# W_in in runs of 256 columns, and x of blocks 1 and 2 in another DMA ring

## The chip, the cores and the metric

The kernel runs on one core of one Trainium2 chip. The metric is device time in microseconds of one execution, the median over several. A core has five engines that run their own instruction streams and meet only through semaphores: TensorE (PE; its weight loads are listed as PEld), VectorE (DVE), ScalarE (ACT), GpSimd (POOL) and SyncE (SP). DMA transfers are issued from an engine's stream. Those that GpSimd issues go through a ring whose descriptors software writes (queue q0 in the profile, "software_dynamic"); those of SyncE and ScalarE go through two rings of the hardware (q1 and q10). All are carried out by the same sixteen DMA engines of the core, and each of the sixteen adds one to the transfer's semaphore when its share has landed. So a wait for 16 is a wait for one whole transfer.

## The reference

A short causal convolution along the sequence with softmaxed taps (8 heads of 24 channels, 7 taps), then a feed-forward layer with the exact GELU:

```python
def _attn_ref(x, weight):                 # x (8, 4096, 192), weight (8, 7)
    w = softmax(weight, axis=-1)
    x_pad = zeros(6 rows) + x             # along the sequence, per batch
    out[b, s, h, g] = sum_k w[h, k] * x_pad[b, s + k, h, g]

def _moe_ref(x, w_in, w_out):             # x (32768, 192), w_in (192, 2048), w_out (2048, 192)
    h = x @ w_in
    g = 0.5 * h * (1.0 + erf(h / sqrt(2)))
    return g @ w_out
```

Here the reference is written shorter than it stands; inputs and output are float32.

## The kernel before

**Tiling.** The 32768 tokens are cut into two halves of 16384, and the two are worked on side by side: half 0 lives in partitions 0 to 63, half 1 in partitions 64 to 127. The 192 channels are three groups (`NP`) of 64. A block is a run of tokens in both halves: blocks 0 to 5 have 256 tokens of each half, the others 512 (`WS`). The 2048 hidden columns are 16 chunks of 128; a chunk pair covers 256 columns, one chunk the even ones and one the odd.

**Stages of a block.** Its x is loaded (`load`, four transfers, by half and by half of the channels) into one of three `xin` buffers. VectorE turns it so that channels lie on partitions (`trans`, line 504). For blocks 0 and 1 the convolution is made on TensorE (`pconv`, line 686) from a bf16 copy (`cast`, by ScalarE for block 0, by GpSimd for block 1) with diagonal weights `dg`; `conv_out` takes it out of PSUM. From block 2 on VectorE makes it, in seven taps with two operations each (lines 525 and 532), the last of which write `xc`. Then `mm1` (line 741) multiplies with W_in into PSUM, ScalarE makes the GELU into `gT` (line 654), and `mm2` (line 772, or `mm2_t`, line 802, for blocks 6 and up) multiplies with W_out. In TensorE's stream the mm2 of the block before stands between the mm1 groups ("units") of a block; a block of 256 tokens has 8 units of two chunks each.

**W_in.** A matmul of a half reads its weights from the same partitions as its tokens, so both halves of the partitions need all of W_in (bf16, converted by the transfer). To read it from memory once, each half is given one part, and VectorE copies it to the other half (`dup`). The parts come in two stages. Before, half 0 owns columns 0 to 1023 and half 1 columns 1024 to 2047; stage 0 is the first 512 columns of each, stage 1 the rest, in runs of 512 columns (2 KB in memory). Half 1 keeps its columns rotated by 1024 (`wcols`). `CH` gives the order in which each half takes the chunks: units 0 and 1 of block 0 need only the half's own stage 0, units 2 and 3 the other half's copied stage 0, units 4 and 5 the stage 1 of half 0 and its copy, units 6 and 7 the stage 1 of half 1 and its copy. The waits for `S_WIN` and `S_DUPE` in `mm1` say this. W_out comes in four parts (`S_WOUT`), each with four chunks. With this `CH` the first sixteen steps of mm2 of block 0 have to be taken in the order `UO`, so that each four of them need one part of W_out.

**Order of the transfers before.** GpSimd's stream: two W_in transfers of stage 0; two of block 1's x (semaphore `S_XP[0]`); wait for the taps (`S_PRO` 9) and the larger part of the diagonal weights (line 397); the other two of block 1's x; two W_in transfers of stage 1; four of W_out; then halo and casts of block 1; four of block 2's x (`S_XP[1]`); halo of the later blocks. SyncE's stream: the taps' weights, half of block 0's x (ScalarE issues the other half); a wait until all of block 2's x has landed (`S_XP[1]`, 64); block 3's x; then, block by block, later x and stores.

**Order of VectorE before.** After the taps: transposes of block 0, its share of `conv_out`, both copies of stage 0 (`dup(0)`), transposes of block 1, both copies of stage 1 (`dup(1)`), `conv_out` of block 1, transposes of block 2, and so on. TensorE does the convolution of block 1 behind the mm1 of units 3 to 6 of block 0:

```python
behind = {(0, 3): p01[:6], (0, 4): p01[6:12], (0, 5): p01[12:] + p2[:6], (0, 6): p2[6:]}
```

Of the kernel before, what the change touches and what calls it, by code (L numbers as in the profile page):

```python
# [11 lines left out]
def bass_lightweight_conv__then__act_gelu_exact_kernel(  # L12
# [9 lines left out]
    D2, F = moe_w_in.shape  # L22
# [60 lines left out]

    CH = [[(8 * hf * (i < 8) + 8 * (i // 4 % 2) + 4 * (i // 8) + i % 4) % NF for i in range(NF)] for hf in range(2)]
    assert all(WS[n] == TB for n in range(M0, NB)) and NG[NB - 1] == 4 and SL0[NB] % 2 == 0

    OUTS = []
# [18 lines left out]
    with es:  # L108
# [24 lines left out]
        S_WIN = [sem("S_WIN%d" % i) for i in range(3)]  # L133
        S_WOUT = [sem("S_WOUT%d" % i) for i in range(4)]
        S_XIN = [sem("S_XIN%d" % i) for i in range(NX)]
        S_XP = [sem("S_XP%d" % i) for i in range(2)]
        S_OUT = [sem("S_OUT%d" % i) for i in range(2)]
        S_MSET = sem("S_MSET")
        S_WNM = sem("S_WNM")
# [69 lines left out]
                e.wait_ge(S_PCE, len(PV) + (1, 3, 6)[p])  # L209

        NCV = 2 * KS
        FH = F // 2
        FP = [0, FH // 2, FH]

        UO = [0, 1, 4, 5, 2, 3, 6, 7]
        UO += [u + 8 for u in UO]

        def cast(e, n, p):
            e.wait_ge(S_TR, NP * n + p + 1)
# [14 lines left out]
            return sum(NCV - 2 * (m in K0) for m in range(n + 1) if m not in PC)  # L234


        def wcols(hf, f):

            return f if hf == 0 else (f + FH) % F

        def xin_at(n):

            return 64 * (n // NX + (n % NX == 0))

        def banks(m, g):

# [122 lines left out]

        @block.gpsimd  # L370
        def _(g):
            def win_in(c0, c1, sm):
                for hf in range(2):
                    g.dma_start(  # L374
                        ap(win, 64 * hf * NP * F + c0, [[NP * F, 64], [F, NP], [1, c1 - c0]]),
                        ap(wint, hf * FH + c0, [[NP * F, 64], [F, NP], [1, c1 - c0]]),
                    ).then_inc(sm[hf], 16)

            g.wait_ge(S_MSET, 1)
            for hf in range(2):  # L380
                m = idb[64 * hf : 64 * hf + 64, :]
                g.affine_select(  # L382
                    out=m,
                    in_=m,
                    compare_op=ALU.is_equal,
                    fill=0.0,
                    base=0,
                    pattern=[[-1, 64]],
                    channel_multiplier=1,
                ).then_inc(S_IDN)  # L390
            g.wait_ge(S_IDN, 2)
            g.memset(wnm[:, :], 0.0).then_inc(S_WNM)  # L392
            g.memset(ap(xTb[0], HF, [[NP * XB, 128], [XB, NP], [1, HB]]), 0.0).then_inc(S_HALO)  # L393
            win_in(FP[0], FP[1], [S_WIN[0]] * 2)
            load(g, 1, (0, 2), S_XP[0])
            g.wait_ge(S_PRO, 9)
            g.tensor_tensor(
                ap(dg, 3 * 64, [[KS * 64, 128], [64, KS - 3], [1, 64]]),
                ap(idb, 0, [[64, 128], [0, KS - 3], [1, 64]]),
                ap(wcol, 3, [[32, 128], [1, KS - 3], [0, 64]]),  # L400
                ALU.mult,
            ).then_inc(S_DG)
            load(g, 1, (1, 3), S_XP[0])
            win_in(FP[1], FP[2], S_WIN[1:])
            for k in range(4):
                g.dma_start(
                    ap(wout, 2 * k * C, [[NF * C, 128], [8 * C, 2], [1, 2 * C]]),
                    ap(woutt, 256 * k * C, [[2 * C, 128], [1024 * C, 2], [1, 2 * C]]),
                ).then_inc(S_WOUT[k], 16)

            def halo(n):

                t, tw = (xTb[PC[n]], XB) if n in PC else (xT[n % 2], XW)
                dst = ap(t, HF, [[NP * tw, 128], [tw, NP], [1, HB]])
                if n >= 4:
                    g.wait_ge(S_CV, cvd(n - 2))
                if OFF[n] % SEQ == 0:
                    g.memset(dst, 0.0).then_inc(S_HALO)
                    return
                g.wait_ge(S_TR, trd(n - 1))  # L420
                src = ap(
                    xT[(n - 1) % 2], HF + WS[n - 1], [[NP * XW, 128], [XW, NP], [1, HB]]
                )
                g.tensor_copy(dst, src).then_inc(S_HALO)  # L424

            halo(1)
            for p in range(NP):
                cast(g, 1, p)
            load(g, 2, sm=S_XP[1])
            halo(2)  # L430
            for n in range(3, NB):
                halo(n)

        @block.vector
        def _(v):
# [22 lines left out]
                    ap(wnt, 4 * (q % 2), [[32, 32], [1, 4], [0, 8]]),  # L458
                ).then_inc(S_PRO)

            def dup(s):

                if s == 0:
                    v.wait_ge(S_WIN[0], 32)
                for hf in range(2):
                    if s == 1:
                        v.wait_ge(S_WIN[1 + hf], 16)
                    v.tensor_copy(
                        ap(
                            win,  # L470
                            64 * (1 - hf) * NP * F + FH + FP[s],
                            [[NP * F, 64], [F, NP], [1, FP[s + 1] - FP[s]]],
                        ),
                        ap(
                            win,
                            64 * hf * NP * F + FP[s],
                            [[NP * F, 64], [F, NP], [1, FP[s + 1] - FP[s]]],
                        ),
                    ).then_inc(S_DUPE)

            def trans(n, p):

                w = WS[n]
                if p == 0:
                    v.wait_ge(S_XP[n - 1] if n in (1, 2) else S_XIN[n % NX], 64 if n in (1, 2) else xin_at(n))
                    if n >= 2 and n - 2 in PC:
                        wait_pc(v, n - 2, NP - 1)
                    elif n >= 2:
                        v.wait_ge(S_CV, cvd(n - 2))
                    if n >= 2:  # L490
                        v.wait_ge(S_HALO, n)
                if n in PC:
                    out = ap(xT[n], p * XW + HX, [[NP * XW, 128], [1, w]])
                    src = ap(
                        xin[n % NX], p, [[TB // 32 * DQ, 128], [DQ, w // 32], [NP, 32]]
                    )
                else:
                    out = ap(xT[n % 2], HX, [[NP * XW, 128], [XW, NP], [1, w]])
                    src = ap(
                        xin[n % NX],  # L500
                        0,
                        [[TB // 32 * DQ, 128], [1, NP], [DQ, w // 32], [NP, 32]],
                    )
                v.transpose(out, src).then_inc(S_TR)  # L504
# [50 lines left out]
                trans(0, p)  # L555
            for j in PV:
                conv_out(v, 0, j)
            dup(0)
            for p in range(NP):
                trans(1, p)  # L560
            dup(1)
            for j in range(len(pieces(1))):
                conv_out(v, 1, j)

# [100 lines left out]
        def _(t):  # L665
# [41 lines left out]
            def mm1(n, i):  # L707
# [19 lines left out]
                for cc, p in todo:  # L727
                    if i == 0 and cc == 0 and p == NP - 1:
                        if n in PC:
                            wait_pc(t, n, p)  # L730
                        else:
                            t.wait_ge(S_CV, cvd(n))
                    for hf in range(2):
                        r = slice(64 * hf, 64 * hf + 64)
                        ch = CH[hf][i * c + cc]
                        f0 = 256 * (ch // 2) + ch % 2
                        fw = 64 if (n == 0 and 4 <= i <= 6) or M0 < n <= M1 else 128
                        for fo in range(0, 128, fw):
                            f1 = 64 * hf * NP * F + p * F + wcols(hf, f0) + 2 * fo
                            o = hf * TB + cc * w  # L740
                            ins = t.matmul(  # L741
                                hp[u % 2][fo : fo + fw, o : o + w],
                                ap(win, f1, [[NP * F, 64], [2, fw]]),
                                xc[n % 2][r, p * TB : p * TB + w],
                                start=(p == 0 and (cc == 0 or not head)),
                                stop=(p == NP - 1 and (cc == c - 1 or not head)),
                                tile_position=(64 * hf, fo),
                            )
                ins.then_inc(S_MM1)

            def mm2(m, g, ph, k):

                i = UO[k] if m == 0 else k
                w = WS[m]
                bb = banks(m, g)
                if k == 0:
# [4 lines left out]
                if g == 0 and ph == 0:  # L761

                    c = NCH[m]
                    if k % 4 == 0:
                        us = range(k, k + 4) if m else UO[k : k + 4]
                        t.wait_ge(S_GELU, SL0[m] + max(us) // c + 1)
                for hf in range(2):
                    sub = ph ^ hf
                    s = 2 * g + sub
# [57 lines left out]
            for n in range(NB):  # L827
                todo = units(n - 1) if n >= 1 else []
                for i in range(NSL[n]):
# [5 lines left out]
                    a0 = len(todo) * sum(ws[:i]) // sum(ws)  # L835
                    a1 = len(todo) * sum(ws[: i + 1]) // sum(ws)
                    for un in todo[a0:a1]:
                        if n == 1 and un[:2] == (0, 0) and un[2] % 4 == 0:
                            t.wait_ge(S_WOUT[un[2] // 4], 16)
                        (mm2_t if new else mm2)(n - 1, *un)  # L840
            m = NB - 1
            for g2 in range(0, NG[m], 2):
# [6 lines left out]
        def _(sp):  # L849
            sp.dma_start(wsb[:, :], ap(wt, 0, [[KS, H], [1, KS]])).then_inc(S_WSB, 16)  # L850
            load(sp, 0, (0, 1))

            sp.wait_ge(S_XP[1], 64)
            load(sp, 3)
            for n in range(1, NB):
                if n + 3 < NB:
# [34 lines left out]
```

## Time and profile before

| what | value |
|---|---|
| median of 4 runs | 681.05 us (680.62 to 682.66) |
| profiled execution, its own time | 680.56 us |
| its span | 678.8 us |
| GELU (line 654) | 512 of 1023 ns on average |
| W_in transfers | 4 of 192 KB (written), median 5.1 us from issue to landing |
| W_out transfers | 4 of 192 KB (written), median 6.9 us |
| x by GpSimd's ring | 8 of 96 KB, median 4.5 us |
| x by SyncE's ring, blocks of 256 tokens | 14 of 96 KB, median 2.4 us |
| granted TensorE clock | 1.00 in each of the first stretches of 8 us |

The span runs from the first to the last instruction that the profiler saw; the 1.76 us by which the execution's own time is longer lie around it. A line of a group names line, engine, operation, what is written from what is read, shapes, and the number of instructions. In the timeline, the first number is the start and the second the length in microseconds, and brackets hold the idle time of the engine before it, with what ended it. An engine name with a small q is the engine's sequencer, which issues transfers. Matmul ends are modelled, so neighbouring lines of TensorE overlap a little.

### The profile page before, as it was taken

To read this page: it belongs to the slowest core of one execution; us is meant where nothing else is said; L and a number is where in the kernel's file an instruction comes from. 1 tells how busy PE (TensorE), PEld (TensorE's weight loads), DVE (VectorE), ACT (ScalarE), POOL (GpSimd) and SP (SyncE) were. 2 spreads that over 40 slices of the span, in tenths; PEclk is the share of its full clock that TensorE was granted. 3 is DMA by queue.
4 is the path that set the end of the run, shared out by engine and by line. 5 is a ranking of instruction groups with operands and counts; after the bars stand their busy time and mean duration, and the time that the engine had idled before them with its cause. 6 is when DMAs were issued, how large, how long until landed. Compare 5 with 4: busy or idle time off the path is not lost.

```text
span 678.8 us, 27140 instructions
## 1 busy us (share of the span) xinstructions
PE 673.7 (99%) x12644; PEld 413.8 (61%) x12644; DVE 527.4 (78%) x607; ACT 536.5 (79%) x550; POOL 35.7 (5%) x62
## 2 busy tenths in 40 slices
PE   8999999999999999999999999999999999999998
PEld 7999655555555555555555555555555555555557
DVE  6989977977779877779777788777797777887511
ACT  8899978787777787787877777877877777778772
POOL 7010000000000000000000000000000000000000
DMA  9335324224443234442234431244422344410123
GB/s 162 98 96 131 71 60 96 53 50 90 95 96 75 52 66 96 95 96 55 51 87 96 95 86 41 65 96 95 96 59 50 84 96 95 92 44 11 48 50 95
DMA packets 131585, 53.66 MB, mean 79 GB/s; under 512 B 125328, under 2 KB 131344, under 8 KB 131472
## 3 DMA queue, kind: packets, MB, share of 16 engines
q1 hardware_dynamic: 128048, 48.97, 31.9%
q0 software_dynamic: 2304, 2.36, 2.1%
q8 instruction: 99, 1.62, 1.0%
q10 hardware_dynamic: 1120, 0.59, 0.3%
q14 instruction: 14, 0.11, 0.1%
HBM read 28.31 MB, written 25.17 MB: 79 GB/s over the span
## 4 chain that ended last, share of the span: by engine, by line
PE 98%; DMA 1%; ACT 1%; POOL 0%; issue 0%; DVE 0%
PE hp L741 49%; PE ob L802 43%; PE ob L772 5%; DMA win<-in_moe_w_in_dram 1%; PE hp L772 1%; ACT gT L654 1%; POOL win L374 0%; POOL idb L382 0%; PE ob L686 0%; DVE osb L293 0%; DVE idb L436 0%; POOL wnm L392 0%; POOL xTb L393 0%
## 5 line engine op out<-in xcount | busy, mean ns | idle before, releaser
L654 ACT ACTIVATE gT<-hp 128x1024 bf16<-128x1024 f32 x512 | 522.7, 1023 | 129.0 <-PE hp L741 125.7
L741 PE MATMUL hp<-xc,win 64*64 64x512 bf16 (+3 forms) x6084 | 419.1, 366 | 1.5 <-DMA win<-in_moe_w_in_dram 0.7
L802 PE MATMUL ob<-gT,wout 64*64 64x512 bf16 x5376 | 366.6, 377 | 0.0
L532 DVE SCALAR_TENSOR_TENSOR acc<-xT,wcol,acc 128x1024 f32<-128x1024 f32 (+1 forms) x330 | 295.6, 947 | 2.9 <-ACT acc L627 2.9
L741 PEld LDWEIGHTS hp<-xc,win 64*64 64x64 bf16 (+1 forms) x6084 | 188.8, 106 | 134.4 <-ACT gT L654 2.0
L802 PEld LDWEIGHTS ob<-gT,wout 64*64 64x64 bf16 x5376 | 173.9, 119 | 121.4
L324 DVE STREAM_TRANSPOSE osb<-ob 128x512 f32<-128x512 f32 x84 | 74.0, 884 | 129.4 <-PE ob L802 129.4
L504 DVE STREAM_TRANSPOSE xT<-xin 128x1536 f32<-128x1536 f32 (+2 forms) x39 | 74.7, 1923 | 1.7 <-DMA xin<-in_x_dram 1.6
L532 DVE SCALAR_TENSOR_TENSOR xc<-xT,wcol,acc 128x1024 bf16<-128x1024 f32 (+1 forms) x66 | 60.4, 954 | 0.0
L424 POOL COPY xT<-xT 128x18 f32<-128x18 f32 x30 | 22.6, 754 | 512.2 <-DVE xT L504 489.6
L772 PE MATMUL ob<-wout,gT 64*128 64x192 bf16 x896 | 46.8, 243 | 0.0
L772 PEld LDWEIGHTS ob<-wout,gT 64*128 64x128 bf16 x896 | 38.7, 94 | 5.1 <-issue 0.4
L525 DVE TENSOR_SCALAR acc<-xT,wcol 128x512 f32<-128x512 f32 (+2 forms) x60 | 33.7, 604 | 1.1
L295 ACT ACTIVATE osb<-ob 128x192 f32<-128x192 f32 x2 | 0.7, 330 | 7.1 <-PE ob L772 7.1
L772 PE MATMUL hp<-wout,gT 64*128 64x192 bf16 x128 | 5.9, 243 | 0.0
L668 PE MATMUL hp<-const-bfloat16-1.0 128*128 128x128 bf16 x48 | 5.0, 301 | 0.8 <-PEq L876 0.8
L293 DVE COPY osb<-ob 128x192 f32<-128x192 f32 x2 | 0.7, 358 | 6.1 <-PE ob L772 6.1
L668 PEld LDWEIGHTS hp<-const-bfloat16-1.0 128*128 128x128 bf16 x48 | 4.9, 142 | 0.8 <-issue 0.8
L772 PEld LDWEIGHTS hp<-wout,gT 64*128 64x128 bf16 x128 | 5.3, 94 | 0.0
L627 ACT ACTIVATE acc<-xT,wcol 128x256 f32<-128x256 f32 (+1 forms) x9 | 5.2, 579 | 0.0
L280 ACT ACTIVATE osb<-ob 128x384 f32<-128x384 f32 x10 | 4.9, 486 | 0.0
L337 POOL DMA_DIRECT2D xin<-in_x_dram x8 | 4.8, 629 | 0.0
(36 smaller groups left out, 32.6 us busy)
## 6 DMA issues: line engine op xcount, KB each, us to landing
out_dram<-osb SPq DMA_DIRECT2D x124, 192.0 KB, 3.1
xin<-in_x_dram SPq DMA_DIRECT2D x116, 192.0 KB, 4.0
xin<-in_x_dram SPq DMA_DIRECT2D x14, 96.0 KB, 2.4
win<-in_moe_w_in_dram POOLq DMA_DIRECT2D x4, 192.0 KB, 5.1
xin<-in_x_dram POOLq DMA_DIRECT2D x8, 96.0 KB, 4.5
wout<-in_moe_w_out_dram POOLq DMA_DIRECT2D x4, 192.0 KB, 6.9
out_dram<-osb ACTq DMA_DIRECT2D x4, 96.0 KB, 2.2
out_dram<-osb SPq DMA_DIRECT2D x4, 96.0 KB, 2.6
```

Source lines behind the costliest of these rows:

```text
L280: e.activation(out=dst, in_=src, func=AF.Copy).then_inc(S_EVA)
L324: v.transpose(ap(osb[m % 2], j, [[8 * C, 128], [C // 2, TB // 32], [NP, 32]]), bank(ring(m, j)),).then_inc(S_EV)
L424: g.tensor_copy(dst, src).then_inc(S_HALO)
L504: v.transpose(out, src).then_inc(S_TR)
L525: ins = v.tensor_scalar(a, src, wk, None, ALU.mult)
L532: ins = v.scalar_tensor_tensor(dst, src, wk, a, op0=ALU.mult, op1=ALU.add)
L627: a.activation(out=acc[n % 2][:, p * TB : p * TB + w], in_=ap(xT[n % 2], p * XW + HX, [[NP * XW, 128], [1, w]]), func=AF.Copy, scale=wcol[ ...
L654: a.activation(out=ap(gT[n % 2], i * c * 2 * w, dst), in_=ap(hp[u % 2], 0, src), func=AF.Gelu,).then_inc(S_GELU)
L668: t.matmul(hp[1][:, 0:128], one, one)
L741: ins = t.matmul(hp[u % 2][fo : fo + fw, o : o + w], ap(win, f1, [[NP * F, 64], [2, fw]]), xc[n % 2][r, p * TB : p * TB + w], start=(p == ...
L772: ins = t.matmul(bb[sub], gT[m % 2][r, c0 : c0 + 128], wout[r, CH[sub][i] * C : (CH[sub][i] + 1) * C], start=(ph == 0 and k == 0), stop=(p ...
L802: ins = t.matmul(bank(ring(m, j), slice(64 * h, 64 * h + 64), w), ap(wout, 64 * hf * NF * C + CH[h][i] * C + j, [[NF * C, 64], [NP, 64]],) ...
```

## The change

Half `hf` now owns, in stage `s`, columns 256 * (2s + hf) to 256 * (2s + hf) + 255 and the same 1024 further on, for each of the three channel groups: six runs of 256 columns (1 KB in memory, 512 B as bf16) per partition, where there were three of 512. The columns lie at the same place in both halves, so `wcols` goes. `CH` is made to fit, and with it mm2 of block 0 takes the chunks in their own order (`UO` goes); its first eight steps need the first two parts of W_out, which are waited for together.

GpSimd's ring carries only weights: two of stage 0, the first of stage 1, (the diagonal weights), the second of stage 1, four of W_out. Block 1's x is issued by SyncE after `S_PRO` 9, and block 2's after the third part of W_out has landed; block 3's follows without a wait of its own on a landing. `S_XP` goes. On VectorE the copies are single steps, and the first of stage 1 stands ahead of the transposes of block 1.

```diff
-    CH = [[(8 * hf * (i < 8) + 8 * (i // 4 % 2) + 4 * (i // 8) + i % 4) % NF for i in range(NF)] for hf in range(2)]
+    CH = [
+        [4 * (i // 8) + 2 * ((i // 4 + hf * (i < 8)) % 2) + 8 * (i // 2 % 2) + i % 2 for i in range(NF)]
+        for hf in range(2)
+    ]
...
+        FQ = F // 8
+        def part(s, hf):
+            return FQ * (2 * s + hf), [[NP * F, 64], [4 * FQ, 2 * NP], [1, FQ]]
...
-            def win_in(c0, c1, sm):
-                for hf in range(2):
+            def win_in(s, sm, hfs):
+                for hf in hfs:
+                    c0, pat = part(s, hf)
                     g.dma_start(
-                        ap(win, 64 * hf * NP * F + c0, [[NP * F, 64], [F, NP], [1, c1 - c0]]),
-                        ap(wint, hf * FH + c0, [[NP * F, 64], [F, NP], [1, c1 - c0]]),
+                        ap(win, 64 * hf * NP * F + c0, pat), ap(wint, c0, pat)
                     ).then_inc(sm[hf], 16)
...
-            win_in(FP[0], FP[1], [S_WIN[0]] * 2)
-            load(g, 1, (0, 2), S_XP[0])
+            win_in(0, [S_WIN[0]] * 2, (0, 1))
+            win_in(1, S_WIN[1:], (0,))
             g.wait_ge(S_PRO, 9)
...
-            load(g, 1, (1, 3), S_XP[0])
-            win_in(FP[1], FP[2], S_WIN[1:])
+            win_in(1, S_WIN[1:], (1,))
...
-            load(g, 2, sm=S_XP[1])
             halo(2)
...
-            dup(0)
+            dup(0, 0)
+            dup(0, 1)
+            dup(1, 0)
             for p in range(NP):
                 trans(1, p)
-            dup(1)
+            dup(1, 1)
...
-                            f1 = 64 * hf * NP * F + p * F + wcols(hf, f0) + 2 * fo
+                            f1 = 64 * hf * NP * F + p * F + f0 + 2 * fo
...
-                i = UO[k] if m == 0 else k
+                i = k
...
-                        us = range(k, k + 4) if m else UO[k : k + 4]
-                        t.wait_ge(S_GELU, SL0[m] + max(us) // c + 1)
+                        t.wait_ge(S_GELU, SL0[m] + (k + 4) // c)
...
-                        if n == 1 and un[:2] == (0, 0) and un[2] % 4 == 0:
-                            t.wait_ge(S_WOUT[un[2] // 4], 16)
+                        if n == 1 and un[:2] == (0, 0) and un[2] in (0, 8, 12):
+                            for q in {0: (0, 1), 8: (2,), 12: (3,)}[un[2]]:
+                                t.wait_ge(S_WOUT[q], 16)
...
-            sp.wait_ge(S_XP[1], 64)
+            sp.wait_ge(S_PRO, 9)
+            load(sp, 1)
+            sp.wait_ge(S_WOUT[2], 16)
+            load(sp, 2)
             load(sp, 3)
```

## The prediction

> **What bounds the kernel now.** I read the page first (busy shares, the forty slices, the chain that ended last), then the chain in order of time over the first 20 us, then the timeline of each engine there, then single DMAs from issue to landing.
>
> ```profile
> span 678.8 us, 27140 instructions
> PE 673.7 (99%) x12644; PEld 413.8 (61%) x12644; DVE 527.4 (78%) x607; ACT 536.5 (79%) x550; POOL 35.7 (5%) x62
> PE   8999999999999999999999999999999999999998
> ```
>
> TensorE is at 99%, and only its first slice (17 us) is less than full. The whole run's list of TensorE's waits holds 1.2 us on data (0.7 on W_in, 0.5 on the GELU), all before 17 us. The change leaves every matmul in number and shape, so the time can move only by when TensorE's unbroken run begins, or by a new hole in it.
>
> The chain in time (start, length, what):
>
> ```profile
> 1.83 0.75 POOL win L374
> 2.58 5.52 DMA win<-in_moe_w_in_dram
> 8.24 0.85 PE hp L741 x12
> 9.11 1.95 ACT gT L654 x2
> ...
> 12.49 0.88 PE hp L741 x24
> 13.39 3.01 ACT gT L654 x3
> 16.44 0.99 PE hp L741 x12
> 17.43 0.66 PE ob L772 x16
> ```
>
> W_in's first two transfers land at 2.58 + 5.52 = 8.10. ScalarE then works through nine GELUs of 1.02 us, with one hole of 0.39 before 13.39. From 17.43 TensorE alternates 0.66 us of mm1 with 0.66 us of mm2 without a hole. What feeds this (timelines of GpSimd, VectorE, SyncE's queue and TensorE; start, length, last bracket the idle time before):
>
> ```profile
> 1.78 1.42 POOL L374 DMA_DIRECT2D win<-in_moe_w_in_dram  x2
> 3.19 1.22 POOL L337 DMA_DIRECT2D xin<-in_x_dram  x2
> 4.70 0.62 POOL L397 TENSOR_TENSOR dg<-idb,wcol 128x256 bf16<-128x256 bf16 x1 [0.29 <-DVE wcol L456]
> 6.43 1.25 POOL L374 DMA_DIRECT2D win<-in_moe_w_in_dram  x2
> 7.68 2.90 POOL L406 DMA_DIRECT2D wout<-in_moe_w_out_dram  x4
> ```
> ```profile
> 9.68 1.34 DVE L504 STREAM_TRANSPOSE xT<-xin 128x256 f32<-128x256 f32 x3
> 11.22 1.13 DVE L468 COPY win<-win 64x1536 bf16<-64x1536 bf16 x1 [0.19 <-DMA win<-in_moe_w_in_dram]
> 13.20 0.81 DVE L468 COPY win<-win 64x1536 bf16<-64x1536 bf16 x1 [0.85 <-DMA win<-in_moe_w_in_dram]
> 18.39 1.23 DVE L504 STREAM_TRANSPOSE xT<-xin 128x768 f32<-128x768 f32 x1 [1.63 <-DMA xin<-in_x_dram]
> ```
> ```profile
> 25.63 1.14 DVE L532 SCALAR_TENSOR_TENSOR xc<-xT,wcol,acc 128x512 bf16<-128x512 f32 x2
> ```
> ```profile
> 27.13 0.82 PE L741 MATMUL hp<-xc,win 64*128 64x256 bf16 x12
> ```
>
> The 18.39 row matters most. Block 2's transpose waits for x2, and from there VectorE runs without a gap until xc of block 2 is whole at 25.63 + 1.14 = 26.77, which is 8.38 us after the landing at about 18.38. TensorE wants that last third at 27.35 (its third pair of matmuls in the group that starts at 27.13). So x2 has only 0.58 us to spare, and every later us of x2 is a us of the end.
>
> **The change, part by part.** All DMAs of these stages landed at (issue plus time to landing, each row asked for alone): W_in 6.40, 8.10, 11.19, 13.17; x1 (block 1) last at 9.52; W_out 14.14, 15.11, 16.22, 17.36; x2 last at 18.37.
>
> *W_in in 1 KB runs.* The bytes are the same, but the packet records, which tell the written size, would show 1536 of 512 B in place of 768 of 1024 B. No 512 B packet of a converting transfer is in the trace. Undisturbed, a 1024 B one takes 96 ns and a 768 B W_out one 78; a straight line through the two gives 60 for 512 B, so 2 x 60 / 96 = 25% more. A transfer is split over sixteen DMA engines and has landed when the last of them is through. On that engine W_in takes about 8.10 - 3.3 (first packet) = 4.8 us for stage 0 and 13.17 - 9.52 = 3.65 for stage 1, so +2.1 us by W_out's time at the most. From below: the W_out rows land 1.0 us apart where W_in's stage 1 lands 1.8 apart; if other addresses brought W_in halfway to W_out's pace, -0.8. I take +0.5, nearer to nothing, since in the trace W_in's packets average 118 ns, so most of their time is not the fixed part that the line shows.
>
> [...]
>
> Issue on GpSimd: x rows of 256 runs take 0.61, W_in of 192 runs 0.62, W_out of 256 runs 0.75. 384 runs cost between 0.62 and twice that. Even doubled, the diagonal multiply (4.70) would end at some 6.2 instead of 5.3, which delays the first convolution (5.83) by 0.4 and hides under TensorE's 0.67 us wait for W_in. Value 0.
>
> *The fourth W_in and W_out move up the ring*, ahead of x1 and x2. The last engine spent 9.52 - 8.10 = 1.42 us on x1: -1.42 for all that follows.
>
> *x1 by SyncE's ring from 4.61* (S_PRO 9). It moves the same 393 KB through the same 16 engines in the same stretch. The nearest row is SyncE's later load of four (20.94 to 24.84 us): 3.9 from first issue to last landing, 0.5 apart. Alone, x1 would land at 4.61 + 3.9 = 8.5; behind all of W_in, at 13.2. I take 11.0. For W_out it costs from 0 (it fills holes) to four steps of 0.45 = 1.8; the packet mean in W_in's stretch (118 against 96) leaves few holes, so +1.6.
>
> [...] The trace has no stretch with both rings full.
>
> *VectorE's order.* The third duplicate goes ahead of block 1's transposes. W_in stage 0 lands at 8.1 + 0.5 = 8.6. The third follows at once in the ring: + 1.67 (11.19 - 9.52) + 0.4 = 10.7. Its duplicate takes 0.81, so the transposes begin at 11.5 instead of 9.68 (x1 at 11.0 does not decide). Transposes and GpSimd's casts take about 1.4 us until the convolution of block 1 can begin: 12.9. It began at 11.86, ahead of mm1 of unit 4 in TensorE's own order, and the GELU at 13.39 hangs on that unit. **Start later by 1.0** (from -1.1 to +2.5).
>
> *x2 behind S_WOUT[2] in SyncE's ring.* Before, GpSimd issued it at 11.67. Now SyncE waits for the third W_out part: 16.22 - 1.42 + 1.6 + 0.5 = 16.9 (14.0 to 18.7). Behind this wait in SyncE's ring stand x3 (needed at 26.7) and later stores, which have room. Four issues and landing take 3.9 (the row above) to 4.6 (18.39 to 22.98); taken 4.1: x2 at 21.0, that is 2.63 late. Less the 0.58 to spare: **+2.05 at block 2**. TensorE arrives there 1.0 late by the start, so the two do not add: the larger counts.
>
> *Nothing for:* the new chunk order, mm2 in straight order, W_out parts 0 and 1 waited for together (15.1 against 17.3; even 1 us later it is hidden, beyond 2.2 TensorE pays), GpSimd freed of four x2 issues (2.40 us in which it had only waits behind).
>
> **Sum.** The profiled execution took 680.56 (span 678.8 and 1.76 around it); + 2.05 = 682.6. It lies 0.49 under the median of the four, so against 681.05: **683.1**.
>
> **Rivals.**
> 1. *x2 is in time, the start alone is late* (x1 held back by the weights, the convolution in front of unit 4): third W_out at 15.3 or sooner, transposes from about 12. For: two loads of one stretch in two rings. Against: x1 has 2 us of room. +1.0 to 2.0, 682.5.
> 2. *The other side: the start is earlier.* Weights alone in the ring, third W_in soon after stage 0, x1 by a quicker queue (2.4 to landing against 4.4 to 4.9 by GpSimd). It takes away the 0.67 before 8.24 and the 0.39 before 13.39: -1.06 at the most, since the convolved x of block 0 is there only at 7.2 to 7.9. 680.0; with half of it 680.5. Decides if stage 0 lands before 7.9, x1 and the third duplicate end before 10.4, and the third W_out lands by 14.8, so that x2 is there at 18.9. For: the engines that are quick had gaps while GpSimd issued. Against: the same bytes pass the same engines.
> 3. *Smaller runs cost much more* (as much per packet as before): stage 0 lands 3 to 4 us later, all after it too, 685 to 688. Against: 384 B packets of x take 22 to 25 ns.
>
> **How the numbers follow.** About 0.2% (1.4 us) is what a measurement can tell here from no change. Forecast 0.55 (0.48 slower, 0.07 within), rival 1 0.15 (0.10, 0.05), rival 2 0.22 (0.18 within, 0.04 faster, since its most is 1.06 us), rival 3 0.08. Together 0.66 slower, 0.30 same, 0.04 faster. The forecast's own range: 681.6 to 685.5. Down to 680.3 for half of rival 2, up to 685.8 for the first of rival 3.
>
> **What would show it.** Step by step: the transposes of block 1 start at about 11.5 and follow a duplicate; the GELU hole before unit 4 grows from 0.39 to above 1; SyncE's load of x2 begins near 16.9; VectorE waits for x2 until about 21; TensorE has a hole of about 1 us before block 2's first group. Wrong if x2 lands by 19, or if the first W_in lands much before or after 8.6.

## The result, and the profile after

The changed kernel is slower: 682.49 us median against 681.26 of the kernel before, ratio 1.0019 with a 95% interval of 1.0011 to 1.0026. Its profiled execution took 681.89 us with a span of 680.1, which is 1.3 more than the 678.8 before. The whole difference is made in the first 19 us.

The chain that ended last, in order of time, of the changed kernel (start, length, what); left-out lines are the taps before and TensorE's run behind:

```profile
4.61 0.31 SPq L336
...
5.95 6.13 DMA xin<-in_x_dram
12.11 0.53 DVE xT L492
12.63 0.05 issue
12.69 0.81 POOL xTb L228 x2
13.50 0.04 issue
13.54 0.52 PE ob L676 x10
14.06 0.68 PE hp L731 x22
14.76 3.01 ACT gT L644 x3
17.78 0.05 issue
17.82 0.93 PE hp L731 x12
18.75 0.66 PE ob L761 x16
```

Before, this chain went through W_in (2.58 to 8.10). Now it goes through the fourth transfer of block 1's x, issued at 5.95 and landed 6.13 us later, at 12.08; then transposes, casts, block 1's convolution and the GELU of unit 4. TensorE's timeline of the changed kernel shows what that costs (in brackets the idle time before, and what ended it):

```profile
13.14 0.92 PE L676 MATMUL ob<-xTb,dg 64*64 64x256 bf16 x12 [1.40 <-POOL xTb L228]
...
18.59 0.82 PE L761 MATMUL ob<-wout,gT 64*128 64x192 bf16 x16
...
28.46 0.82 PE L731 MATMUL hp<-xc,win 64*128 64x256 bf16 x12
```

The first mm2 was at 17.27 and is at 18.59, 1.32 later, and nothing of it is won back. In ScalarE's timeline the hole before the GELU of unit 4 has grown from 0.39 to 1.95 us:

```profile
14.76 5.06 ACT L644 ACTIVATE gT<-hp 128x1024 bf16<-128x1024 f32 x5 [1.95 <-PE hp L731]
```

VectorE's timeline has the other half:

```profile
8.21 1.73 DVE L465 COPY win<-win 64x1536 bf16<-64x1536 bf16 x3
12.11 1.33 DVE L492 STREAM_TRANSPOSE xT<-xin 128x256 f32<-128x256 f32 x3 [2.17 <-DMA xin<-in_x_dram]
...
20.22 1.23 DVE L492 STREAM_TRANSPOSE xT<-xin 128x768 f32<-128x768 f32 x1 [2.14 <-DMA xin<-in_x_dram]
...
27.47 1.13 DVE L520 SCALAR_TENSOR_TENSOR xc<-xT,wcol,acc 128x512 bf16<-128x512 f32 x2
```

The first three of the four copies of W_in are through at 9.94, and VectorE waits 2.17 us for x1. It waits again for x2, which landed at 20.20 (18.37 before); xc of block 2 is whole at 28.60. TensorE came 1.33 later to block 2 as well (group at 28.46, last third wanted at 28.68), so x2's delay of 1.83 was just covered, with 0.08 us left.

The landings, before and after: W_in 6.40, 8.10, 11.19, 13.17, now 6.18, 7.92, 9.07, 11.87; third W_out 16.22, now 14.82; x1 complete 9.52, now 12.08. The weights became earlier, x later.

### The profile page after: what moved, and what is told of

Read it like the earlier page. It is cut to its first block, busy times and chain, and to the rows that moved or that the text cites. A ratio compares the mean times of both kernels' runs of the same rounds, so it can differ in the third digit from the quotient of the medians.

```text
span 680.1 us, 27138 instructions
## 1 busy us (share of the span) xinstructions
PE 674.0 (99%) x12644; PEld 413.9 (61%) x12644; DVE 526.1 (77%) x607; ACT 536.7 (79%) x550; POOL 32.1 (5%) x54
## 4 chain that ended last, share of the span: by engine, by line
PE 97%; DMA 1%; ACT 0%; DVE 0%; SPq 0%; POOL 0%; issue 0%; ACTq 0%
PE hp L731 48%; PE ob L791 43%; PE ob L761 5%; DMA xin<-in_x_dram 1%; PE hp L761 1%; ACT gT L644 0%; DMA wsb<-in_weight_dram 0%; SPq L336 0%; DVE wcol L453 0%; POOL xTb L228 0%; DVE xT L492 0%; PE ob L676 0%; DVE osb L292 0%; ACT wex L580 0%; DVE wnm L444 0%
## 5 line engine op out<-in xcount | busy, mean ns | idle before, releaser
L676 PE MATMUL ob<-xTb,dg 64*64 64x256 bf16 (+1 forms) x112 | 4.1, 246 | 1.5 <-POOL xTb L228 1.4
L202 DVE CAST xc<-ob 64x256 bf16<-64x256 f32 (+3 forms) x8 | 2.9, 357 | 3.1 <-PE ob L676 2.9
```

Source lines behind the costliest of these rows:

```text
L676: ins = t.matmul(bank(kd, slice(64 * ho, 64 * ho + 64), w), dg[r, d0 : d0 + 64], xTb[PC[n]][r, x0 : x0 + w], start=(k == KS - 1), stop=(k ...
```

## The experiments

In the runs below the kernel before was timed beside them; ratios are against it.

**layout_alone.** The runs of 256 columns without the new transfer order; the third copy stands behind block 1's transposes again. Its diff against the changed kernel, shortened:

```diff
-            win_in(1, S_WIN[1:], (0,))
+            load(g, 1, (0, 2), S_XP[0])
...
-            win_in(1, S_WIN[1:], (1,))
+            load(g, 1, (1, 3), S_XP[0])
+            win_in(1, S_WIN[1:], (0, 1))
...
+            load(g, 2, sm=S_XP[1])
...
-            sp.wait_ge(S_PRO, 9)
-            load(sp, 1)
-            sp.wait_ge(S_WOUT[2], 16)
-            load(sp, 2)
+            sp.wait_ge(S_XP[1], 64)
             load(sp, 3)
```

> The runs of 256 columns, the new chunk order and the single copies, but every transfer in the ring and the order of before. Theory (the whole loss comes from x1 waiting in SyncE's ring behind the weights): block 1's transposes start at 9.7 as before, stage 0 of W_in lands at 7.7 to 8.1, span 678.3 to 679.0, ratio 0.999 to 1.001. Rival (the smaller runs cost something): stage 0 or the third W_in land later than 8.10 and 11.19, span 679.3 or more, ratio above 1.001.

Ratio 0.9995 (0.9987 to 1.0004), stage 0 landed at 7.45, the third W_in at 10.91, and block 1's transposes began at 9.61. The smaller runs cost nothing that can be measured. Only the span, 679.3, lies outside the theory's range, because of something new. TensorE's timeline of this kernel:

```profile
13.06 0.74 PE L734 MATMUL hp<-xc,win 64*64 64x256 bf16 x19
14.31 0.38 PE L734 MATMUL hp<-xc,win 64*64 64x256 bf16 x5 [0.51 <-issue]
```

It stops inside unit 5, after 19 of 24 matmuls, for nothing that the profile shows. (x1_back below starts block 1 alike and has no such stop; its first mm2 is at 17.04, that of this kernel at 17.63.) More of this under x_then_w_warm.

**x1_early.** SyncE's wait for the taps in front of x1 is left out.

> The changed kernel, but SyncE issues block 1's x at once behind its half of block 0's, near 2.1 us, without the wait for the taps. Theory (two limits, x1 in front and x2 0.1 us behind it): x1 lands before 8, block 1's transposes follow the third copy near 10, the GELU hole before unit 4 shrinks from 1.95 to under 0.5; but x2 still waits for the third W_out and lands near 20, so TensorE stops about 1.3 us before block 2 and the span stays at 679.8 to 680.4, ratio 1.001 to 1.003. Rival (x1 alone is the cause): span 678.8 or less, ratio 1.000 or below.

Ratio 1.0004 (0.9996 to 1.0013), span 679.9. The span lies in the theory's range, but neither mechanism fits. x1 took its turns with W_in: its transfers landed at 6.02, 7.62, 9.28 and 10.52, W_in's at 7.22, 8.90, 10.67 and 11.73, one after the other. So the first mm1 waited for stage 0 until 9.04, and the first mm2 of the profiled execution came at 18.37. Block 2 was then again not held up by x2 (19.86). What x1 gained, W_in lost.

**x2_early.** `sp.wait_ge(S_WOUT[2], 16)` becomes `S_WOUT[0]`.

> The changed kernel, but block 2's x waits for the first part of W_out instead of the third (issue near 12.4 instead of 14.84). Theory: x2 lands 1 us or more sooner, VectorE finishes block 2's xc before 27.6, and nothing comes of it: span 679.8 to 680.3, ratio 1.001 to 1.003. Rival (the forecast: x2 sets the end): span 679 or less, ratio at or under 1.0005.

Ratio 1.0027 (1.0015 to 1.0039, eight runs). x2 landed at 17.85 instead of 20.20, and nothing came of it: x2 did not set the end of the changed kernel. The profiled execution caught something else, and its span, 682.3, lies above both ranges for that reason; TensorE's clock by windows (us, busy, granted clock, DMA share, GB/s):

```profile
12.00:13.00 1.00, 0.00 (x0) 1.00 1.31 199
...
14.00:15.00 1.00, 0.97 (x18) 0.50 1.19 224
15.00:16.00 1.00, 1.00 (x26) 0.50 1.03 245
16.00:17.00 1.00, 1.00 (x24) 0.50 0.90 207
17.00:18.00 1.00, 1.00 (x44) 0.80 0.95 204
```

x1 came still later here (12.83), TensorE idled 2.21 us, and from 14.0 to 17.4 it ran on half its clock.

**both_early.** Both edits.

> Both edits together. Theory (two limits in a row): only this one gains, span 677.6 to 678.8, ratio 0.998 to 1.000, with no hole of TensorE before block 2. Rival (x1 alone is the cause): same as x1_early within 0.2 us. Rival (early x takes from W_in's stage 0 what it gains): stage 0 lands after 8.8, span 679.3 or more.

Ratio 1.0005 (0.9997 to 1.0014), span 679.9, as x1_early; stage 0 landed at 8.96. The numbers of both rivals fit, the theory's do not: as long as x1 and W_in only change places, there is no earlier start for x2 to spoil.

**x1_back.** layout_alone with only x2 in SyncE's ring behind the third W_out.

```diff
-            load(g, 2, sm=S_XP[1])
...
-            sp.wait_ge(S_XP[1], 64)
+            sp.wait_ge(S_WOUT[2], 16)
+            load(sp, 2)
```

> layout_alone, but block 2's x goes by SyncE's ring behind the third W_out, as in the changed kernel; block 1's x stays in the software ring. Theory (x2 is a limit of its own, right behind x1): block 1 starts as in layout_alone, x2 lands near 20.3 instead of 18.65, TensorE stops 0.8 to 2 us before block 2, span 680.0 to 681.2, ratio 1.0015 to 1.0035. Rival (x2 never matters): span 679.3 and ratio 0.999 to 1.001 as layout_alone.

Ratio 1.0009 (1.0001 to 1.0018), span 680.1. TensorE's timeline at block 2:

```profile
28.29 0.92 PE L733 MATMUL hp<-xc,win 64*128 64x256 bf16 x12 [1.21 <-DVE xc L522]
```

With x1 in time (9.23) the first mm2 is at 17.04, and then x2, landed at 20.13, opens a hole of 1.21 us. So x2's new place is by itself a limit at block 2, as the prediction said, though it costs 1.21 us and not 2.05; in the changed kernel x1's delay covers it. The ratio is below the expected 1.0015.

**turn_first.** The changed kernel with block 1's transposes ahead of the third copy.

> The changed kernel with block 1's transposes ahead of the third copy on VectorE, as it was before. Theory (x1 lands last at 12, two microseconds after that copy): transposes again near 12.1, third copy now behind them, GELU hole 1.9 or more, span 680.0 to 680.8, ratio 1.0015 to 1.003. Rival (the forecast: the copy in front sets the transposes): transposes start 0.8 sooner than in the changed kernel, span 679.4 or less, ratio 1.0005 or less.

Ratio 1.0034 (1.0022 to 1.0046, six runs), above the expected 1.003; span 680.1, and the first mm2 at 18.61, as in the changed kernel. The transposes began at 11.78, after 2.54 us of waiting for x1, which landed at 11.75. The copy in front was not what held them up.

**x1_third_step.** The changed kernel with `sp.wait_ge(S_PRO, 3)` for 9, and x2 behind the first W_out.

> The changed kernel with two waits moved and nothing else: SyncE issues block 1's x from 3.2 us (third step of the taps instead of the ninth, 4.61), block 2's x waits for the first W_out. The third W_in transfer still goes ahead of the diagonal weights, and its copy ahead of block 1's transposes. Theory (block 1's x in front of stage 1 of W_in is all that counts, and 1.4 us of earlier issue give it a turn sooner): all of x1 lands by 10.7, the convolution of block 1 begins by 12.4, span 678.8 to 679.6, ratio 0.9990 to 1.0005, so part of x_then_w's gain. Rival (x1 is served only once the weights queued before it are through): x1 after 11.5, span 679.8 or more, ratio 1.001 or more.

Ratio 1.0003 (0.9995 to 1.0012), span 679.4, convolution of block 1 at 12.45. x1 was complete at 11.38: 0.7 better than in the changed kernel, not the 1.4 by which it was issued earlier, so between the theory's 10.7 and the rival's 11.5. The last of its four transfers still came behind the third of W_in (9.77).

**x_then_w.** As x1_third_step, and moreover both W_in transfers of stage 1 are issued behind the diagonal weights, and the transposes stand ahead of the third copy (this last move is not in the lines below, which are against the changed kernel).

```diff
-            win_in(1, S_WIN[1:], (0,))
             g.wait_ge(S_PRO, 9)
...
-            win_in(1, S_WIN[1:], (1,))
+            win_in(1, S_WIN[1:], (0, 1))
...
-            sp.wait_ge(S_PRO, 9)
+            sp.wait_ge(S_PRO, 3)
             load(sp, 1)
-            sp.wait_ge(S_WOUT[2], 16)
+            sp.wait_ge(S_WOUT[0], 16)
             load(sp, 2)
```

> The layout of the changed kernel with x ahead of the second stage of W_in: SyncE issues block 1's x from 3.2 us (third step of the taps), GpSimd issues both W_in transfers of stage 1 behind the diagonal weights, VectorE turns block 1's x ahead of the third copy, and block 2's x waits for the first W_out. Theory (x1 and W_in share one bandwidth, what counts is the order of need): x1 lands by 10, stage 0 by 8.6, the convolution of block 1 begins by 11.7, no hole before block 2, span 678.2 to 679.0, ratio 0.998 to 1.000. Rival (rings take turns, whatever the order of issue): x1 after 10.5 or stage 0 after 9, span 679.5 or more.

Landings as expected (stage 0 at 8.09, x1 at 9.62; the third W_in at 10.21), block 1's convolution at 11.85 instead of by 11.7, and the profiled execution has a span of 678.4. But the ratio is 0.9998 (0.9987 to 1.0008): executions lie between 679.68 and 683.40.

**x_then_w_warm.** The warm-up as 24 matmuls of 512 columns.

> x_then_w, with the 48 warm-up matmuls of 128 columns as 24 of 512 (24 fewer pairs of instructions for TensorE before its next 16 KB of code, about the same time). Theory (the unexplained stop inside unit 5 in layout_alone, x1_early and both_early is code that waits in the same DMA engines): the stop is gone or comes a unit later with less than 0.3, span 0.3 to 0.6 below x_then_w, ratio 0.997 to 0.999. Rival (the stop has another cause): it stays at the same matmul, span as x_then_w within 0.2.

Ratio 1.0021 (1.0012 to 1.0030). As a kernel it is slower: the wide matmuls took 0.28 us each, 6.7 in all, and held up the convolution until 8.73. But they tell where the stop comes from. TensorE's timeline:

```profile
16.18 0.45 PE L676 MATMUL ob<-xTb,dg 64*64 64x256 bf16 x16
16.50 0.30 PE L731 MATMUL hp<-xc,win 64*64 64x256 bf16 x3
17.13 0.84 PE L731 MATMUL hp<-xc,win 64*64 64x256 bf16 x21 [0.33 <-issue]
```

It stops after 3 matmuls of unit 6, for 0.33 us (under 0.3 was expected). Counted from the program's start (24 + 56 + 48 + 12 + 24 + 12 + 24 + 16 + 3) that is after 219 matmuls. In layout_alone, x1_early and both_early it is after 219 as well (48 + 56 + 48 + 12 + 24 + 12 + 19). The place is one in TensorE's instruction stream. The DMA records hold packets of 16,384 B in the queue of kind "instruction", the first of which runs at 8.59 in the kernel before, at 12.00, 12.72 and 12.71 in those three, and at 14.68 here; TensorE goes on 1.35 to 1.50 us after that packet's end each time. In x_then_w's profiled execution it ran at 10.21, and there is no stop. So the stop belongs to a place in the code and ends a nearly fixed time behind the packet; that TensorE waits for this packet is the reading that fits both.

**x_then_w_96.** The warm-up as 96 matmuls of 64 columns, which by that reading moves TensorE's need of the next code into the first convolution.

```diff
-            for i in range(48):
-                t.matmul(hp[1][:, 0:128], one, one)
+            small = nc.const_aps.tensor(1.0, (128, 64), BF16)
+            for i in range(96):
+                t.matmul(hp[1][0:64, 0:64], small, small)
```

> x_then_w with 96 warm-up matmuls of 64 columns in place of 48 of 128 (48 more pairs of instructions, about the same 5 us), so that TensorE asks for its next 16 KB of code earlier, during the first convolution instead of the first mm1. Theory (the spread of x_then_w, 679.7 to 682.4, is that load coming late in some executions): the load is seen before 9, executions lie within 1 us of each other, median 679.9 to 680.5, ratio 0.998 to 0.9992. Rival (the spread has another cause): spread and median as x_then_w, ratio 0.999 to 1.001.

Ratio 0.9991 (0.9982 to 0.9999), median 680.42, all eleven executions between 680.02 and 680.85. The packet ran at 9.05, which is 0.05 behind what was expected. This version beats both kernels, the one before by 0.1%, just clear of the interval. That the narrow spread comes from the earlier packet is not shown: x_then_w ran beside a kernel before that itself lay between 680.54 and 684.03, this one beside 680.15 to 682.07, x_then_w's slowest execution has a lowered clock (more under filler), and no slow execution of it was profiled. VectorE's timeline:

```profile
8.08 1.14 DVE L464 COPY win<-win 64x1536 bf16<-64x1536 bf16 x2
9.39 1.33 DVE L491 STREAM_TRANSPOSE xT<-xin 128x256 f32<-128x256 f32 x3 [0.17 <-DMA xin<-in_x_dram]
10.76 0.56 DVE L464 COPY win<-win 64x1536 bf16<-64x1536 bf16 x1
```

x1 and the weights arrive in the order in which VectorE wants them, with waits of 0.17, none, and 0.52 for the fourth copy, where the changed kernel waited 2.17 for x1.

**before_96.** The kernel before with that warm-up.

> The kernel before, with nothing changed but the 96 warm-up matmuls of 64 columns. Theory (the code load also catches some executions of the kernel before, and the transfer order gives the rest of x_then_w_96's gain): the runs draw together, none above 681.6, median 680.5 to 680.9, ratio 0.9992 to 1.0000, the profile's span 678.6 to 679.0 as before. Rival (all of x_then_w_96's gain is the code load): median 680.4 or less, span 678.4 or less, ratio 0.9991 or less.

Ratio 1.0007 (0.9998 to 1.0016), span 679.8: neither. The 16 KB packet ran at 8.75 for 1.18 us. Of the 64 increments of x1's semaphore 63 were there by 9.54, the last one at 11.24; VectorE's transposes began at 11.27 instead of 9.68:

```profile
11.27 1.36 DVE L504 STREAM_TRANSPOSE xT<-xin 128x256 f32<-128x256 f32 x3 [1.50 <-DMA xin<-in_x_dram]
```

So the gain of x_then_w_96 is not the warm-up alone. That the code packet held up the engine with the last increment is read from the coincidence; the records do not name engines.

**filler.** Twelve matmuls on constants where the changed kernel's TensorE is idle.

> The changed kernel with 12 more matmuls of 128x128 on constants, into a corner of PSUM that nobody reads, in front of block 1's convolution, where TensorE sits idle. They leave the result alone. Theory (in about a third of the executions of the changed kernel x1 is so late that the idle stretch makes the granted clock drop, which costs 2 us more): the granted clock is 1.0 or 0.999 in all executions, none is above 683.3, median 681.8 to 682.3, ratio 1.0010 to 1.0017. Rival (the idle stretch has nothing to do with it): executions near 684 with a mean clock of 0.997 stay, ratio 1.0019 or more.

Ratio 1.0018 (1.0006 to 1.0030). Ten of twelve executions had a mean clock of 1.0, two still 0.997 and 0.998 at 684.18 and 684.74. Of the changed kernel's 45 executions 16 show 0.997 or 0.998 (one 0.999 aside) and take 682.7 to 685.3. The share fell, but two of twelve against 16 of 45 settles nothing, and the expectation was missed. All runs together say more: in the four kernels whose profile has x1 complete at 11.75 or later (the changed one, x2_early, turn_first, filler) 22 of 71 executions have a mean clock of 0.998 or less, in the other nine and the kernel before beside them 3 of 206. So a late x1 and the lowered clock go together, though no run shows how. Without its 16 such executions the changed kernel's median is 682.20, so they make some 0.3 of the 1.23 us of loss.

## Why the prediction was right in sign and range, and wrong in its cause

**What bounds the kernel: right.** The matmuls took the same time (TensorE busy for 673.7 us before, 674.0 now); the start alone moved the end (the first mm2 came 1.32 later, the span grew by 1.3).

**W_in in 1 KB runs: mis-sized.** Taken at +0.5; stage 0 landed 0.18 earlier (0.65 in layout_alone, 0.17 in x1_back, which starts alike, so the most of that 0.65 is scatter). The straight line was good: 59 ns for the quickest 512 B packet, against 60. Over all of W_in a 512 B packet took 70 ns on average and a 1024 B one before 121, so the W_in packets together took 16% longer (12% in layout_alone), not 25%: what slowed the packets beyond their quickest, 25 ns at 1024 B and 11 at 512 B, went with the bytes and not with the number. That the landings did not follow even these 16% is measured, its reason is open. A value of 0 would have been the better one. (The first W_in packet before ran at 3.47, not at 3.3; that moves the +2.1 by 0.04.)

**Issue on GpSimd at nothing: right.** 384 runs cost 0.66 against 0.62.

**x1's bytes at +1.6 on W_out: wrong side.** The third W_out landed at 14.82 where 16.9 was forecast. That is 1.40 earlier than before, where the move up the ring alone was put at 1.42. The forecast let the weights pay for x1 in a ring of its own; x1 paid alone.

**x1 at 11.0: too early.** It was 12.08. From issue to landing its four transfers took 4.5 to 6.1 us by SyncE's ring, where GpSimd's had taken 3.4 to 4.4 before (not the 4.4 to 4.9 of the second rival, which are those of x2); the 2.4 us of SyncE's other loads come from stretches with less traffic (DMA share 0.52 from 18.4 to 23.0 us before, 1.29 from 4.6 to 12.1 us now). The shares of the two rings changed from one microsecond to the next: between 8 and 9 us the trace has 644 records of x against 74 of W_in, between 9 and 10 it has 121 against 313.

**VectorE's order as the cause of the late start: wrong.** The third copy was through at 9.94, x1 decided, and turn_first shows it. The size, +1.0, was near the measured 1.32 by luck.

**x2 at 21.0 and +2.05 at block 2: the step that failed.** x2 landed at 20.20, 0.8 sooner than forecast, from two errors that partly cancel: it was issued 2.06 sooner (14.84) and took 5.36 us instead of 4.1, since one of SyncE's issues took 1.80 instead of 0.45 (more in the last section). Its lateness of 1.83 less the 0.58 to spare is 1.25, and the start was 1.32 late. "The larger counts" was the right rule, and the larger was the start, by less than 0.1 us. TensorE has no hole before block 2, which the prediction had named as its sign; its sign of being wrong, x2 by 19, did not show either. This is the first rival's mechanism, x1 held back by the weights; its price was 682.5, and 682.49 was measured. x1_back shows that x2 stood right behind with 1.21 us. So it is partly luck that the time fell into the forecast's range: the sum had +2.05 from x2, and the measured +1.23 came from x1.

**"No gain over 1.06": held.** The best version gains some 0.7 us (interval 0.1 to 1.2).

## What to carry to other kernels

Here a transfer that was moved to another ring still competed with those it had left: what x1 gained by an earlier issue (complete at 10.52 instead of 12.08) W_in's stage 0 lost (8.90 instead of 7.92; x1_early). What was wanted first had to be issued first, over both rings: with its own issue from 3.2 us, x1 was complete at 11.38 where the third W_in followed stage 0 at once (x1_third_step), at 9.62 where that one came behind the diagonal weights (x_then_w). Before moving a load, list each stage's landings beside the moment at which each is wanted; a second limit that lies 0.1 us behind the first can hide what the first is worth, and its own repair alone gains nothing (x2_early). When two kernels of the same work differ in spread rather than in their best time, look at the granted clock of each execution, and at the transfers that the program does not issue itself, code among them.

## What the runs showed of the hardware that was not expected

- Code comes in packets of 16,384 B (queue q8 of the profile, kind "instruction", 99 packets, 1.1% of the time of the 16 DMA engines in the changed kernel). The first one after the program's start ran between 7.60 (x1_back) and 14.68, in the kernel before at 8.59; that it waits in the queue as the other rings' loads do is likely but not shown, as its request is not recorded. In four profiles in which it ran at 12.0 or later TensorE stopped at its 220th matmul for 0.23 to 0.51 us; in the changed kernel, where it ran at 12.16, TensorE came to that matmul only at 15.32 and did not stop.
- SyncE issues a load or store in some 0.5 us (median 0.49 in the changed kernel), but single issues took 1.2 to 2.0. In the changed kernel's profile all 23 that took over 1 us overlap one of the 16 KB packets in time, of its other 243 issues only 33 do. One of the 23 is the issue in x2's load (15.68 to 17.48; the packet ran from 15.72 to 17.09). Why was not tried.
- One idle stretch of 2.21 us (x2_early) was followed by 3.4 us at half the granted clock, while one of 1.40 us in the changed kernel's profiled execution left the clock at 1.00. In the twelve traces that record changes of the clock, each stretch between two changes is a whole multiple of 3.413 us (3, 1 and 195 of them in x2_early, 198 in the changed kernel). In the step before the drop, 10.57 to 13.98, TensorE was busy for 1.11 us; in the changed kernel's steps around its idle stretch, 9.17 to 12.59 and 12.59 to 16.00, for 2.03 and 2.75. That this decides was not tested.
- A copy of 64 x 1536 bf16 on VectorE took 0.55 us at its quickest with six runs of 256 (all four of the changed kernel) and 0.69 with three of 512 (all four of before_96). Why was not tried.
